# Zero products in an attention's gaps, a fetch of sums put ahead, a flag read early

## The chip, the cores and the metric
One Trainium2 chip, one of its cores. The metric is the device time of one execution in microseconds (us), as the median of several runs. TensorE (PE in the profile) multiplies matrices into PSUM, VectorE (DVE), ScalarE (ACT) and GpSimd (POOL) work on vectors, and SyncE (SP) issues most transfers between HBM and the core's memory.

## The reference
A sparse attention feeds a gated feed-forward layer (FFN 1), and that a second one (FFN 2). All is float32.

```python
scores = scale * np.matmul(q, k.transpose(0, 1, 3, 2))      # batch 4, 8 heads, 576 positions, 64 wide
scores = np.where(masks[None, :, :, :], scores, -1000000000.0)   # window of 32, in half the heads with step 4
...
attn = attn / (np.sum(attn, axis=-1, keepdims=True) + 1e-09)
return np.matmul(attn, v).astype(np.float32)

g = x @ w_gate                                               # 2304 x 512 @ 512 x 1536
silu = g * (1.0 / (1.0 + np.exp(-g)))
val = x @ w_val
return (silu * val @ w_out).astype(np.float32)

h = x @ w_in                                                 # 2304 x 512 @ 512 x 2048
g = h - np.tanh(h)
return (g @ w_out).astype(np.float32)
```

## The kernel before
**Order.** All work is put into a `Plan` as tasks: an engine, an estimated duration, a priority, what it depends on, and the buffers that it needs (rings of a fixed size: eight PSUM buffers `ps`, four of sums `acc`, two of raw weights `st`, six of `q`, eight of `v`). `Plan.order()` plays the tasks through with these estimates: an engine that is free takes the ready task with the lowest priority number whose buffers are free. The result fixes the order of instructions on each engine and in SP's queue, and which buffer each task gets. On the chip each engine then keeps its order and waits by semaphores. A task that is added or gets another dependency can so move others.

**Attention.** 48 units (4 batches, 4 pairs of heads, 3 groups of 192 queries). Each one: loads of q (with k) and v, three score products (L330), maxima and exponentials, normalisation on GpSimd, three transposes (L355), six products with V (L368), and copies into `x`. "Score set 16" is the L330 work of unit 16, and so on. Ten bf16 products of a tile of zeros (`warm_up`, L700) stand ahead of the first unit.

**FFN 1 and 2.** Six tiles of 384 tokens in three pairs. Weights are loaded as 64-bit words and converted (L249 to L265). Each float32 product is made of three products of high and low parts. One pair is done plainly (`plain_up`, L404), two pairs with seven products in place of eight (`product`, L416). Products with the output weights are L582 (FFN 1) and L601 (FFN 2). The hidden width is taken in groups of chunks; after each group, partial sums go to HBM (`add_up`: store by SP or accumulating store by GpSimd). In the last group the sums are fetched back (L539) into an `acc` buffer, VectorE adds the last products to them (L550), and in FFN 2 the result is stored to the output (L614). The last tile's final output is cut in two halves of 256 columns.

**The flag.** FFN 2 uses a cubic in place of h - tanh(h). Whether every value was small enough for that is counted (`count`, `across`, `tell`), and a flag is read into a register on each engine (L883); a branch (L884) leads to `any_size`, which computes FFN 2 again, or past it.

The dependency of the fetch, as it stands:

```python
fetched = plan.add("DMA", 2.0, prio - 6.0, lambda: nc.sync.dma_start(out=at(), in_=keep),
                   [sum_done[t], pieces[0][4][0]], [at], lat=5.0)
```

`pieces[0][4][0]` is the first hidden tile (`y`) of the same token tile: the fetch isn't planned before that is ready.

Of the kernel before, what the change touches and what calls it, by code (L numbers as in the profile page):

```python
# [21 lines left out]
P = 128  # L22
# [145 lines left out]
CONV0 = -18.6  # L168
LEAD = 25.0
DELAY = 10.0  # L170
ON_DVE = {(2, 1)}
DELAY_7 = 6.0
MM = 0.174
QUICK = 0.6
WARM = 10
# [6 lines left out]
def attention_then_two_ffns(ctx, tc, qk, vt, masks, w1, w2, out):  # L182
    nc = tc.nc
# [7 lines left out]
    plan = Plan({r: n for r, (n, _) in SLOTS.items()})  # L191
# [12 lines left out]
    new_ps = ring("ps", [P, 512], F32)  # L204
# [20 lines left out]
    warm = const.tile([P, 512], mybir.dt.bfloat16, name="warm")  # L225
# [168 lines left out]
    covered = {}  # L394
# [136 lines left out]

    sum_done = [None] * NT

    def add_up(layer, t, pieces, first, last, prio):

        at = new_acc()
        keep = sums[layer - 1][t]
        if last:
            fetched = plan.add("DMA", 2.0, prio - 6.0, lambda: nc.sync.dma_start(out=at(), in_=keep),  # L539
                               [sum_done[t], pieces[0][4][0]], [at], lat=5.0)  # L540
        puts = []
        for n, (mm, c0, c1, dur, deps, bufs) in enumerate(pieces):
            ps = new_ps()

            eng = "DVE" if last or (layer, n) in ON_DVE else "ACT"

            def put(ps=ps, c0=c0, c1=c1, eng=eng):
                o = at()[:, c0:c1]
                if last:
                    nc.vector.tensor_tensor(out=o, in0=ps()[:, :c1 - c0], in1=o, op=ALU.add)  # L550
                elif eng == "DVE":
                    nc.vector.tensor_copy(out=o, in_=ps()[:, :c1 - c0])
                else:
                    nc.scalar.activation(out=o, in_=ps()[:, :c1 - c0], func=AF.Copy)  # L554

            a = plan.add("PE", dur, prio, lambda mm=mm, ps=ps: mm(ps), deps, [ps] + bufs)
            c = (c1 - c0) / 1000
            if last:
                a = plan.add("DVE", 0.15 + 1.08 * c, prio, put, [a, fetched], [ps, at])
            else:  # L560
                a = plan.add(eng, 0.15 + 1.08 * c if eng == "DVE" else 0.18 + 0.84 * c, prio, put, [a], [ps, at])
            puts.append(a)
        if last:
            return at, puts

        def store():
            if first:
                nc.sync.dma_start(out=keep, in_=at())
            else:
                nc.gpsimd.dma_start(out=keep, in_=at(), accum_op=ALU.add)  # L570

        sum_done[t] = plan.add("DMA" if first else "POOL", 2.0 if first else 1.3, prio - 5.0, store, puts + [sum_done[t]], [at],
                               lat=8.0)
# [14 lines left out]
                           [w[2][0] for w in ws] + [y for y, _ in ys]))  # L588
        return add_up(1, t, pieces, first, last, prio)

    def ffn2_out(ws, ys, t, first, last, prio, end=False):
        pieces = []
        cuts = [(s, 0, DM) for s in range(NS)]
        if end:
            cuts[-1:] = [(NS - 1, 0, DM // 2), (NS - 1, DM // 2, DM)]
        for s, c0, c1 in cuts:
            def mm(ps, s=s, c0=c0, c1=c1):
                n = 0
                for w, y in zip(ws, ys):
                    for a, bb in PASSES:  # L600
                        nc.tensor.matmul(ps()[:, :c1 - c0], lhsT=y[0]()[:, a, s * P:(s + 1) * P],  # L601
                                         rhs=w[1][0]()[:, bb, c0:c1], start=(n == 0), stop=(n == 3 * len(ws) - 1))
                        n += 1
                covered[ps.slot] = c1 - c0

            pieces.append((mm, s * DM + c0, s * DM + c1, MM * 4 * len(ws) * (c1 - c0) / DM,
                           [d for _, d in ys] + [w[1][1] for w in ws], [w[1][0] for w in ws] + [y for y, _ in ys]))
        r = add_up(2, t, pieces, first, last, prio)
        if last:
            at, puts = r  # L610
            for (s, c0, c1), a in zip(cuts, puts):
                def store(s=s, c0=c0, c1=c1):
                    r0 = t * TT + s * P
                    nc.sync.dma_start(out=out[r0:r0 + P, c0:c1], in_=at()[:, s * DM + c0:s * DM + c1])  # L614

                plan.add("DMA", 0.75 * (c1 - c0) / DM, -1e6, store, [a], [at])
# [53 lines left out]
    def seven_next(p, r, prio):  # L670

        (r1, d1), (r2, d2) = r
        seven_x[p] = sums_x(r1, r2, d1 + d2, None, prio)
# [22 lines left out]
    ps_warm = new_ps()  # L696
# [2 lines left out]
        for _ in range(WARM):  # L699
            nc.tensor.matmul(ps_warm(), lhsT=warm[:, :P], rhs=warm, start=True, stop=True)  # L700

    plan.add("PE", 0.43 * WARM, -1e6, warm_up, bufs=[ps_warm])
    n = 0
    for b in range(B):
        for hp in range(NP):
# [14 lines left out]
    def finish(layer, h, prio):  # L720
        if layer == 1:
            (g, a), v = h
            return times_val(times_gate(g, a, prio), v, prio)
        (h, a), = h
        return cubic(h, a, prio)
# [4 lines left out]
    flag = const.tile([P, 1], mybir.dt.int32, name="flag")  # L730
    when = 0.0
    for layer, sizes in ((1, GROUPS1), (2, GROUPS2)):
        k = 0
        for n in sizes:
            first, last = k == 0, k + n == (NK1, NK2)[layer - 1]
            src, parts = ((w1, 3), (w2, 2))[layer - 1]
            lead = when - LEAD if k or layer == 2 else CONV0
            ups = range(parts - 1)
            sevens = SEVEN if n == 2 else []
            ws = [[None] * parts for _ in range(n)]  # L740
            extra = [None] * parts
            for c in range(parts):
                for i in range(n):
                    ws[i][c] = convert(src[k + i][:, c * 512:(c + 1) * 512], lead + 2 * c, layer == 1 and k == 0)
            for c in ups:
                if sevens:
                    extra[c] = sums_w(ws[0][c], ws[1][c], lead + 6 + 2 * c)
            if layer == 1 and k == 2:
                for p in SEVEN:
                    seven_first(p, when)  # L750
            outp = (ffn1_out, ffn2_out)[layer - 1]
            order = [0, 1, 2] if layer == 1 and not last else [1, 2, 0]
            for p in order:
                tiles = PAIRS[p]
                ys = {t: [] for t in tiles}
                if p in sevens:
                    q = [seven_up(ws[0][c], ws[1][c], extra[c], p, when + 0.01 * c) for c in ups]
                    res = {(i, t): [q[c][2 * i + j] for c in ups] for i in range(2) for j, t in enumerate(tiles)}
                    ys = {t: [None, None] for t in tiles}
                    for i, t in [(0, tiles[0]), (0, tiles[1]), (1, tiles[1]), (1, tiles[0])]:  # L760
                        ys[t][i] = finish(layer, res[i, t], when + 0.02)
                    when += (14.6, 7.3)[layer - 1]
                    for t in tiles:
                        done = outp(ws, ys[t], t, first, last, when + DELAY_7)
                        when += 2.09 * n
                        if last and layer == 1:
                            after[t] = done
                else:
                    for t in tiles:
                        ys = []  # L770
                        for w in ws:
                            ys.append(finish(layer, [plain_up([w], c, t, when)[0] for c in ups], when))
                            when += (4.18, 2.09)[layer - 1]
                        end = {"end": True} if layer == 2 and last and p == order[-1] and t == tiles[-1] else {}
                        done = outp(ws, ys, t, first, last, when + DELAY, **end)
                        when += 2.09 * n
                        if last and layer == 1:
                            after[t] = done
                if last and layer == 1:
                    if p in SEVEN:  # L780
                        seven_next(p, [after[t] for t in tiles], when + DELAY)
                    else:
                        for t in tiles:
                            plain_next(t, after[t], when + DELAY)
            k += n
# [6 lines left out]
    ps_flag = new_ps()  # L792
# [7 lines left out]

    a = plan.add("DVE", 0.4, -1e6, count, squares)
    a = plan.add("PE", 0.3, -1e6, across, [a], [ps_flag])
    plan.add("DVE", 0.1, -1e6, tell, [a], [ps_flag])


    def any_size():
# [73 lines left out]
    with tc.manual_schedule():  # L880
        for t in plan.order():
            t.emit()
        bad = nc.values_load(flag[0:1, 0:1], min_val=0, max_val=1)  # L883
        with tc.If(bad > 0):  # L884
            any_size()


# [48 lines left out]
```

## Time and profile before

| | |
|---|---|
| median of 3 runs | 925.24 us (923.45 to 928.22) |
| the profiled execution | 928.41 us, span 926.3 us from first to last instruction |
| TensorE busy | 904.8 us, 98% of the span |
| VectorE busy | 638.1 us, 69% |
| ScalarE busy | 519.0 us, 56% |
| GpSimd busy | 300.5 us, 32% |
| mean granted TensorE clock | 0.985 of full |
| moved by DMA | 134.55 MB, mean 145 GB/s |

Busy means that an instruction is in flight; matrix products are pipelined, and their ends are modelled. The granted clock is the share of full speed that TensorE was given. The chain of waits, followed back from the last instruction, lies on TensorE for 90% of the span.

### The profile page before, as it was taken

How to read it: one execution, taken by the hardware profiler on the slowest of the kernel's cores; microseconds unless marked ns; L12 is line 12 of the kernel's file. 1: busy time of each engine (PE TensorE's matmuls, PEld its weight loads, DVE VectorE, ACT ScalarE, POOL GpSimd, SP SyncE). 2: the span in 40 equal slices, each digit the busy share in tenths (PEclk: the TensorE clock that was granted, in tenths of full speed). 3: DMA queues.
4: the chain of work that ended last, by engine and by line, in shares of the span. 5: the costliest groups of instructions: out<-in, count | busy, mean ns of one | idle time of the engine just before them, and what ended most of it. 6: DMA issues, size and time to landing. Idle time of an engine off the chain costs nothing.

```text
span 926.3 us, 15209 instructions
## 1 busy us (share of the span) xinstructions
PE 904.8 (98%) x5418; PEld 854.4 (92%) x5418; DVE 638.1 (69%) x1428; ACT 519.0 (56%) x1379; POOL 300.5 (32%) x298
## 2 busy tenths in 40 slices
PE   7899999999999999999999989999999999999996
PEld 6789999999999999999999988899898998999994
DVE  4688888854833833943867998985868585946373
ACT  5598876745645544644655556655656555545430
POOL 2334434314413512522514222242525242521100
PEclk8799999999999999999999999999999999999998
DMA  9887744862672672572581304568685857574756
GB/s 274 233 265 258 252 123 69 204 149 41 141 160 35 137 170 35 128 180 35 115 242 54 114 23 144 197 137 161 140 163 122 165 137 145 106 128 77 171 169 210
DMA packets 38005, 134.55 MB, mean 145 GB/s; under 512 B 4384, under 2 KB 9248, under 8 KB 37920
## 3 DMA queue, kind: packets, MB, share of 16 engines
q0 software_dynamic: 9504, 51.91, 31.4%
q1 hardware_dynamic: 28416, 81.57, 27.5%
q8 instruction: 45, 0.74, 0.3%
q14 instruction: 40, 0.33, 0.1%
HBM read 67.40 MB, written 66.06 MB: 144 GB/s over the span
## 4 chain that ended last, share of the span: by engine, by line
PE 90%; DVE 5%; DMA 3%; SPq 1%; issue 0%; ACT 0%; DVEq 0%
PE ps L416 27%; PE ps L601 21%; PE ps L404 20%; PE ps L582 14%; PE ps L330 3%; PE ps L368 2%; PE ps L355 2%; DMA q<-qk 2%; DVE x L631 1%; DVE acc L550 1%; DVE acc L646 1%; DMA acc<-sum 1%; DVE x L684 0%; DMA st<-w 0%; DVE y L483 0%; DVE t L520 0%
## 5 line engine op out<-in xcount | busy, mean ns | idle before, releaser
L416 PE MATMUL ps<-x,wc 128*128 128x384 f32 x1512 | 279.3, 337 | 0.4 <-DVE acc L550 0.4
L416 PEld LDWEIGHTS ps<-x,wc 128*128 128x128 f32 x1512 | 266.2, 188 | 3.3 <-DVE acc L550 0.7
L237 POOL TENSOR_TENSOR wc<-u,wc 128x512 fp32r<-128x512 f32 x104 | 149.0, 1438 | 224.9 <-ACT wc L234 209.2
L404 PE MATMUL ps<-x,wc 128*128 128x384 f32 x1152 | 210.7, 336 | 0.6 <-DVE t L523 0.6
L601 PE MATMUL ps<-wc,y 128*128 128x512 f32 (+1 forms) x870 | 204.0, 389 | 0.0
L404 PEld LDWEIGHTS ps<-x,wc 128*128 128x128 f32 x1152 | 200.4, 188 | 1.6 <-DVE t L523 0.9
L601 PEld LDWEIGHTS ps<-wc,y 128*128 128x128 f32 x870 | 162.1, 188 | 32.1
L554 ACT ACTIVATE acc<-ps 128x384 f32<-128x384 f32 (+1 forms) x228 | 118.3, 529 | 108.0 <-PE ps L601 56.1
L582 PE MATMUL ps<-y,wc 128*128 128x384 f32 x864 | 159.8, 336 | 1.8 <-DVE acc L550 0.9
L582 PEld LDWEIGHTS ps<-y,wc 128*128 128x128 f32 x864 | 150.5, 188 | 2.8 <-DVE acc L550 1.2
L483 DVE TENSOR_TENSOR y<-t,y 128x384 fp32r<-128x384 f32 x168 | 122.0, 732 | 35.3 <-ACT y L479 34.9
L570 POOL DMA_DIRECT2D sum<-acc x66 | 58.1, 880 | 264.0 <-ACT acc L554 194.5
L234 ACT ACTIVATE wc<-u 128x512 fp32r<-128x512 f32 x104 | 65.5, 630 | 72.3 <-PE ps L416 31.5
L479 ACT ACTIVATE y<-t 128x384 fp32r<-128x384 f32 x168 | 86.2, 519 | 35.2 <-PE ps L601 20.9
L520 DVE SCALAR_TENSOR_TENSOR t<-t 128x384 f32<-128x384 f32 x96 | 63.4, 665 | 29.7 <-ACT t L517 29.7
L456 DVE TENSOR_TENSOR ps<-ps,t 128x384 f32<-128x384 f32 x36 | 20.4, 566 | 65.1 <-PE ps L416 65.0
L252 ACT ACTIVATE u<-st 128x512 f32<-128x512 f32 x68 | 45.2, 667 | 33.3 <-DMA st<-w 32.8
L349 POOL TENSOR_TENSOR e<-e,sm 128x288 f32<-128x288 f32 x48 | 34.4, 720 | 80.0 <-DVE sm L346 27.6
L341 ACT ACTIVATE e<-e,nm 128x96 f32<-128x96 f32 x144 | 52.1, 371 | 8.2 <-DVE nm L335 8.0
L495 DVE SCALAR_TENSOR_TENSOR t<-t,ps 128x384 f32<-128x384 f32 x62 | 34.0, 549 | 28.9 <-ACT t L492 28.4
L427 ACT ACTIVATE ps<-ps 128x384 f32<-128x384 f32 x72 | 34.3, 477 | 34.8 <-PE ps L416 34.7
L260 DVE SCALAR_TENSOR_TENSOR u<-st,u 128x512 uint32<-128x512 uint32 x68 | 53.2, 782 | 0.6
(61 smaller groups left out, 859.5 us busy)
## 6 DMA issues: line engine op xcount, KB each, us to landing
sum<-acc POOLq DMA_DIRECT2D x66, 768.0 KB, 7.1
st<-w SPq DMA_DIRECT2D x68, 512.0 KB, 4.5
q<-qk SPq DMA_DIRECT2D x48, 304.0 KB, 5.1
sum<-acc SPq DMA_DIRECT2D x12, 768.0 KB, 5.6
acc<-sum SPq DMA_DIRECT2D x12, 768.0 KB, 6.1
v<-vt SPq DMA_DIRECT2D x48, 144.0 KB, 4.7
out<-acc SPq DMA_DIRECT2D x17, 256.0 KB, 2.9
mask<-masks SPq DMA_DIRECT2D x1, 288.0 KB, 4.5
```

Of the source, the lines that this page charges most:

```text
L234: nc.scalar.activation(out=w()[:, 0, :], in_=u(), func=AF.Copy)
L237: nc.gpsimd.tensor_tensor(out=w()[:, 1, :], in0=u(), in1=w()[:, 0, :].bitcast(F32), op=ALU.subtract)
L260: nc.vector.scalar_tensor_tensor(out=ui, in0=words(0, U32), scalar=29, in1=ui, op0=ALU.logical_shift_right, op1=ALU.bitwise_or)
L404: nc.tensor.matmul(ps()[:, :TT], lhsT=w()[:, a, kc * P:(kc + 1) * P], rhs=xt[kc // 2]()[:, bb, kc % 2, :], start=(n == 0), stop=(n == 3 * ...
L416: nc.tensor.matmul(ps()[:, :TT], lhsT=w()[:, i, c:c + P], rhs=b()[:, j, k, :], start=(start and n == 0), stop=(n == 5), skip_group_check=True)
L479: nc.scalar.activation(out=y()[:, 0, :], in_=s(), func=AF.Copy)
L483: e.tensor_tensor(out=y()[:, 1, :], in0=s(), in1=y()[:, 0, :].bitcast(F32), op=ALU.subtract)
L520: nc.vector.scalar_tensor_tensor(out=sq(), in0=sq(), scalar=E0 / E1, in1=sq(), op0=ALU.add, op1=ALU.mult)
L554: nc.scalar.activation(out=o, in_=ps()[:, :c1 - c0], func=AF.Copy)
L570: nc.gpsimd.dma_start(out=keep, in_=at(), accum_op=ALU.add)
L582: nc.tensor.matmul(ps()[:, :TT], lhsT=w[2][0]()[:, a, m * P:(m + 1) * P], rhs=y[0]()[:, bb, :], start=(n == 0), stop=(n == 3 * len(ws) - 1))
L601: nc.tensor.matmul(ps()[:, :c1 - c0], lhsT=y[0]()[:, a, s * P:(s + 1) * P], rhs=w[1][0]()[:, bb, c0:c1], start=(n == 0), stop=(n == 3 * le ...
```

## The change
Three things. (1) Thirty tasks `fill` of two products of zeros each (the tile `warm`, into a PSUM buffer that nobody reads) are added to TensorE's plan with the highest priority number, each dependent on the one before; the plan puts one wherever it sees TensorE without other work. (2) In FFN 2's last group, the fetch of a tile's sums no longer depends on that tile's own first `y`, but on the first `y` of the pair that was done before (`early`). (3) The flag is read into registers in a task of the plan, right behind `tell`; the branch stays at the end.

```diff
+FILL = 30
...
-    def add_up(layer, t, pieces, first, last, prio):
+    def add_up(layer, t, pieces, first, last, prio, early=None):
...
             fetched = plan.add("DMA", 2.0, prio - 6.0, lambda: nc.sync.dma_start(out=at(), in_=keep),
-                               [sum_done[t], pieces[0][4][0]], [at], lat=5.0)
+                               [sum_done[t], early or pieces[0][4][0]], [at], lat=5.0)
...
-    plan.add("PE", 0.43 * WARM, -1e6, warm_up, bufs=[ps_warm])
+    ps_warmed = plan.add("PE", 0.43 * WARM, -1e6, warm_up, bufs=[ps_warm])
...
+            early = None
             for p in order:
...
+                    now_early = ys[tiles[0]][0][1]
                     for t in tiles:
-                        done = outp(ws, ys[t], t, first, last, when + DELAY_7)
+                        more = {"early": early} if layer == 2 and last else {}
+                        done = outp(ws, ys[t], t, first, last, when + DELAY_7, **more)
...
+                if p in sevens:
+                    early = now_early
...
-    plan.add("DVE", 0.1, -1e6, tell, [a], [ps_flag])
+    a = plan.add("DVE", 0.1, -1e6, tell, [a], [ps_flag])
+    verdict = []
+    plan.add("NONE", 0.0, -1e6, lambda: verdict.append(nc.values_load(flag[0:1, 0:1], min_val=0, max_val=1)), [a])
+
+
+    a = ps_warmed
+    for _ in range(FILL):
+        ps = new_ps()
+
+        def fill(ps=ps):
+            for _ in range(2):
+                nc.tensor.matmul(ps(), lhsT=warm[:, :P], rhs=warm, start=True, stop=True)
+            covered[ps.slot] = 512
+
+        a = plan.add("PE", 0.46, 1e6, fill, [a], [ps], lat=0.5)
...
-        bad = nc.values_load(flag[0:1, 0:1], min_val=0, max_val=1)
-        with tc.If(bad > 0):
+        with tc.If(verdict[0] > 0):
             any_size()
```

Where the instructions stand. Numbers behind a name tell buffers in use apart and differ between the two kernels; line numbers of the changed kernel are one higher from L331 on, and its fills are L822.

TensorE in the attention, before the change: from score set 15 to score set 19 (L330), with the transposes of units 10 and 11 (L355) and the V products of unit 10 (L368) between them.

```order
L330 MATMUL ps_512<-q_466 128x96 x3
L355 MATMUL ps_527<-ident,e_456 96x128 x3
L330 MATMUL ps_543<-q_485 128x96 x3
L368 MATMUL ps_561<-at_550,v_347 64x64 x6
L330 MATMUL ps_570<-q_508 128x96 x3
L330 MATMUL ps_590<-q_540 128x96 x3
L355 MATMUL ps_599<-ident,e_502 96x128 x3
L330 MATMUL ps_603<-q_552 128x96 x3
```

The same place after the change: score sets 16 to 18 (L331). Just ahead of these rows stand the V products of units 9 and 10 and two more fills, just behind them one more fill and the transposes of unit 11.

```order
L331 MATMUL ps_580<-q_520 128x96 x3
L822 LDWEIGHTS warm
L822 MATMUL ps_598<-warm 128x512
L822 LDWEIGHTS warm
L822 MATMUL ps_598<-warm 128x512
L331 MATMUL ps_607<-q_548 128x96 x3
L822 LDWEIGHTS warm
L822 MATMUL ps_617<-warm 128x512
L822 LDWEIGHTS warm
L822 MATMUL ps_617<-warm 128x512
L331 MATMUL ps_623<-q_577 128x96 x3
```

Each score set from 16 to 18 now has a fill behind it, and V set 10 has moved ahead of score set 16. Thirteen fills stand between score sets 2 and 19; between score sets 13 and 15 there is none.

TensorE at the boundary of the layers, before: FFN 1's last seven-product blocks (L416) and the output products behind them (L582).

```order
L416 MATMUL ps_6120<-x_5882,wc_6055 128x384 x6
L416 MATMUL ps_6095<-x_5886,wc_5647 128x384 x6
L416 MATMUL ps_6134<-x_5985,wc_5822 128x384 x6
L582 MATMUL ps_6168<-y_6052,wc_5392 128x384 x3
L582 MATMUL ps_6168<-y_6132,wc_5607 128x384 x3
```

After, the same L417 products (L416 before):

```order
L822 LDWEIGHTS warm
L822 MATMUL ps_6187<-warm 128x512
L417 MATMUL ps_6137<-x_5925,wc_5686 128x384 x6
L417 MATMUL ps_6182<-x_6024,wc_5861 128x384 x6
L822 LDWEIGHTS warm
L822 MATMUL ps_6213<-warm 128x512
L822 LDWEIGHTS warm
L822 MATMUL ps_6213<-warm 128x512
```

Three fills now stand ahead of these two blocks and two behind them; nine in all at this boundary, six of them ahead of the L582 products above.

SP's queue at the end, before: fetches of sums (L539) and stores of the output (L614); `acc_9742` is the last tile's.

```order
L614 DMA out<-acc_9497 128x512 x2
L614 DMA out<-acc_9431 128x512
L539 DMA acc_9603<-sum 128x1536
L614 DMA out<-acc_9431 128x512 x2
L539 DMA acc_9633<-sum 128x1536
L614 DMA out<-acc_9497 128x512
L614 DMA out<-acc_9603 128x512 x2
L614 DMA out<-acc_9633 128x512 x2
L614 DMA out<-acc_9557 128x512 x3
L539 DMA acc_9742<-sum 128x1536
```

After (L540 and L615; `acc_9717` is the last tile's, `acc_9696` the one that was `acc_9603`):

```order
L540 DMA acc_9567<-sum 128x1536
L615 DMA out<-acc_9567 128x512 x2
L615 DMA out<-acc_9497 128x512 x3
L540 DMA acc_9696<-sum 128x1536
L615 DMA out<-acc_9567 128x512
L540 DMA acc_9717<-sum 128x1536
L615 DMA out<-acc_9696 128x512 x2
L813 TENSOR_LOAD flag
L813 ISA x2
L615 DMA out<-acc_9531 128x512 x2
```

The last fetch now stands behind six stores, before behind thirteen; the fetch for the sum that the next products belong to stands behind five, before behind three. The flag's read stands among the stores. On TensorE it stands two output pieces of FFN 2 behind `across` and eight ahead of the end, where it was last before; three fills stand ahead of the run of output pieces that ends the program, two ahead of the last tile's four, and three behind them.

## Rows read from the trace of the kernel before

**Rows 1.** Busy time by stage: stretch, length, busy per engine, PEclk, DMA share, GB/s.
```profile
11.40:18.20 6.80, 6.08 (x37) 5.54 (x37) 3.70 (x28) 3.93 (x19) 2.80 (x5) 0.50 1.04 298
...
28.00:35.20 7.20, 4.49 (x50) 3.57 (x48) 5.32 (x37) 4.43 (x22) 4.06 (x4) 1.00 0.96 276
35.20:48.90 13.70, 12.55 (x81) 11.57 (x81) 7.43 (x49) 6.58 (x33) 4.07 (x5) 0.50 0.66 206
48.90:145.00 96.10, 95.93 (x964) 88.98 (x961) 80.09 (x388) 79.44 (x343) 38.45 (x46) 1.00 0.71 218
...
500.00:556.00 56.00, 53.29 (x300) 51.83 (x299) 55.66 (x90) 32.64 (x65) 14.74 (x11) 1.00 0.18 57
...
880.00:917.00 37.00, 37.00 (x186) 32.73 (x184) 24.69 (x49) 10.27 (x29) 0.00 (x0) 1.00 0.66 214
```

**Rows 2.** Waits of SP's DMA queue, 35 to 50 us: total, times, longest.
```profile
SPq L372 <- PE ps L368: 10.0, 3, 4.9
```

**Rows 3.** TensorE in order of time, attention: start, length, idle before.
```profile
36.35 1.57 PE L330 MATMUL ps<-q 128*128 128x96 f32 x6 [1.37 <-DMA q<-qk]
```

**Rows 4.** The chain that ended last, in order of time: start, length, what.
```profile
38.76 2.81 PE ps L330 x12
...
44.71 0.84 PE ps L368 x12
45.55 0.81 PE ps L355 x3
...
68.76 0.64 PE ps L330 x6
69.40 0.50 PE ps L368 x12
69.90 0.46 PE ps L355 x3
...
852.54 12.28 PE ps L601 x54
```

**Rows 5.** The tile of zeros: duration min/median/max in ns, first and last start.
```profile
L700 PE MATMUL ps<-warm x10: 379/634/634, 1.2 to 4.8; 128*128 128x512 bf16 x10
```

**Rows 6.** TensorE in order of time at the boundary of the layers.
```profile
537.68 1.33 PE L582 MATMUL ps<-y,wc 128*128 128x384 f32 x6 [0.88 <-DVE t L523]
...
540.97 1.32 PE L582 MATMUL ps<-y,wc 128*128 128x384 f32 x6 [0.91 <-DVE acc L550]
```

**Rows 7.** The chain that ended last, its end.
```profile
900.36 5.49 PE ps L601 x24
...
911.34 6.33 DMA acc<-sum
...
918.95 0.75 DVE acc L550 x2
```

**Rows 8.** All engines in order of time from 880 us.
```profile
894.29 0.37 SPq L539 DMA_DIRECT2D acc<-sum  x1
...
900.87 0.33 SPq L539 DMA_DIRECT2D acc<-sum  x1
...
901.29 10.00 SPq L614 DMA_DIRECT2D out<-acc  x8
...
905.83 11.25 PE L601 MATMUL ps<-wc,y 128*128 128x512 f32 x54
```

**Rows 9.** Line 883, the flag's read: duration in ns, first and last start.
```profile
L883 PEldq TENSOR_LOAD <-flag x1: 516/516/516, 914.1 to 914.1; - x1
...
L883 SPq TENSOR_LOAD <-flag x1: 485/485/485, 920.6 to 920.6; - x1
```

**Rows 10.** Line 884, the branch and the waits after it.
```profile
L884 SPq EVENT_SEMAPHORE  x8: 17/17/17, 924.1 to 924.6; - x8
...
L884 SPq COMPARE_BRANCH  x1: 50/50/50, 921.5 to 921.5; - x1
```

**Rows 11.** Line 614 from 919.8 us, the last two stores.
```profile
DMA to landing us min/median/max: 3.6/3.7/3.8
```

More of the change, by code (lines that the diff above doesn't have):

```diff
@@ L589, in ffn1_out, with ffn2_out @@
         return add_up(1, t, pieces, first, last, prio)
-    def ffn2_out(ws, ys, t, first, last, prio, end=False):
+    def ffn2_out(ws, ys, t, first, last, prio, end=False, early=None):
         pieces = []
@@ L607, in ffn2_out @@
                            [d for _, d in ys] + [w[1][1] for w in ws], [w[1][0] for w in ws] + [y for y, _ in ys]))
-        r = add_up(2, t, pieces, first, last, prio)
+        r = add_up(2, t, pieces, first, last, prio, early)
         if last:
@@ L773, in attention_then_two_ffns @@
                             when += (4.18, 2.09)[layer - 1]
-                        end = {"end": True} if layer == 2 and last and p == order[-1] and t == tiles[-1] else {}
-                        done = outp(ws, ys, t, first, last, when + DELAY, **end)
+                        more = {"early": early} if layer == 2 and last else {}
+                        if layer == 2 and last and p == order[-1] and t == tiles[-1]:
+                            more["end"] = True
+                        done = outp(ws, ys, t, first, last, when + DELAY, **more)
                         when += 2.09 * n
```

## The prediction
> **What bounds the kernel now.** I read the busy time by stage first [rows 1]. From 48.9 us on, TensorE has something in flight practically all the time at the full granted clock: 95.93 of 96.10 us up to 145 us and 37.00 of 37.00 at the end; of the later stages only 500 to 556 us shows a gap, 53.29 of 56.00 us. What TensorE is given there is paid in full, except in that gap. The reader should look at two other rows of the group. In the attention the clock is granted at 0.50 of full (1.2 of 2.4 GHz) twice, from 11.4 to 18.2 us and from 35.2 to 48.9 us. The first costs nothing that I can find: the DMA share there is 1.04, transfers set the pace, and TensorE still waits for them later. The second is different. The DMA share drops to 0.66, although loads for the scores are still to come. The DMA queue's own waits say why: it stands 10.0 us behind the products with V that free a V buffer [rows 2]. TensorE at half clock is the bound there, and everything later hangs on it.
>
> What TensorE did before that fall is the row of 28.0 to 35.2 us in [rows 1]: busy 4.49 of 7.20 us, with short waits for q such as the 1.37 us at 36.35 [rows 3].
>
> Then the chain of work at either level [rows 4]: two sets of scores take 2.81 us at half clock, one takes 0.64 at full; a set of products with V 0.84 and 0.50; a set of transposes 0.81 (in others 0.64) and 0.46. Last come the end's rows [rows 7 to 11].
>
> **The change part by part.**
>
> *Price of one fill.* A fill is two bf16 products of 512 columns. The ten warm-up products start between 1.2 and 4.8 us, 0.40 us apart [rows 5]; the full-clock price is that of the 512-column L601 products, 12.28 us for 54, 0.227 each [rows 4]. So a fill is 0.46 us at full clock and 0.80 us at the slow pace. In the order, thirty fills fall as 13 in the attention, 9 at the boundary of the layers, 5 ahead of the last outputs, and 3 after the last output product.
>
> *Attention, if the clock stays up.* The chain from 36.35 to 49.05 us holds six sets of scores (8.1 us in all), three sets of products with V (2.5) and three sets of transposes (2.1). At the full-clock prices that is 3.9, 1.5 and 1.4 us: 5.9 us less. Can the transfers feed that? They run at 276 GB/s before the fall and 206 in the slow stretch [rows 1], so 0.96 MB, or 3.5 us of transfer, is lost in those 13.7 us; it comes back if V buffers are freed sooner. Against it stand the fills. The first eight and the two ahead of score set 16 lie in waits for q; three more lie between score set 16 and the transposes after set 18, 1.4 us, hidden only where TensorE waits for q. Ends: -5.9 (all hidden) and -4.5 (three paid); I take -4.6, since TensorE shows next to no wait after set 16 today, so only a transfer that is late for the faster TensorE could hide them. If the cover is gone and the clock falls anyway, the five fills from set 16 on cost 0.80 each, 4.0 us, less the 1.37 us of wait: +2.6.
>
> Does the clock stay up? The fills do not lie evenly in the stretch that goes before the fall: between score sets 13 and 15 there is none; two follow just before set 16. One thing helps besides: in the new order two loads (V 14 and q 15) pass the third weight load, so score set 15 comes sooner. I give 6 to 7 in 10 that the slow stretch goes, and 2.5 in 10 that it comes but ends sooner, since a fill at the slow pace is 0.80 us without a break.
>
> *Boundary of the layers.* Nine fills, 4.1 us. TensorE's gaps there are 2.7 us in all (56.00 - 53.29), the longest 0.88 and 0.91 us, both for VectorE [rows 6], which is busy 55.66 of 56.00 us [rows 1]. Six fills stand ahead of the first of them, so they eat it and delay TensorE into the next. If VectorE loses nothing by that, 4.1 - 2.7 = 1.4 us remain; if TensorE's delay reaches VectorE's operands each time, all 4.1. I take +1.8, near the lower end because VectorE's queue is full of work that does not depend on these products (a row with 0.34 us of idle time). The clock is 1.00 here already: there is nothing to win.
>
> *End, TensorE.* Five fills ahead of the last outputs, in a stretch without a gap [rows 1]: paid, +2.3 us (0 only if the new order leaves them a wait; today's has none). The flag's read now stands in the middle of TensorE's output products. Its queue took 0.52 us for it at 914.1 us [rows 9] while products ran to 905.83 + 11.25 = 917.08 [rows 8], so the queue issues some 3 us ahead, and a pause of 0.5 us alone should not reach the array. Bounds 0, and 0.52 plus what the flag is late: I take +0.5, the flag being late for the reason below. The Trainium skill (TensorE: Matmul & The Clock Gate, architectural detail on the array, engine queue depths) gives TensorE a queue of 64 against 8 elsewhere. By that the read would cost nothing; the trace's lead of 3 us agrees.
>
> *End, the early fetch.* Today the sixth and last fetch of sums goes at 911.34 us and lands 6.33 us later; the last additions end at 918.95 + 0.75 = 919.70 [rows 7], while the last product ends at 917.08. In the new order it stands behind six stores instead of thirteen and takes the buffer of the sixth's sum. That store goes at about 901.29 [rows 8]; a landing takes 3.6 to 3.8 us [rows 11]; so the fetch goes at about 905.5 and is there at 912, before it is needed. The additions then end some 0.6 us after the last product, 917.7 instead of 919.70: -2.0. What is late next? The sum that the next products belong to, fetched fourth at 894.29 today, becomes the fifth, which waits for a store to land and goes at 900.87 [rows 8]. With 6.3 us it lands at 907, while its first products (six take 1.37, 5.49 / 4 [rows 7]) are done at 900.36 + 1.4 + 1.4 = 903.1. VectorE stands up to 4 us, and behind it the flag and the other additions; TensorE has eight PSUM buffers, and VectorE's 0.7 us per addition against 1.37 of products catches up before the last tile. Cost 0 beyond the 0.5 above, or up to 1 if a PSUM buffer lacks.
>
> *End, the flag.* On SP the read starts at 920.6 us [rows 9] and the branch at 921.5; the eight waits after it run from 924.1 to 924.6 [rows 10]. Without the read the branch comes 0.86 us sooner, and the waits with it, the last at 923.8. The last two stores go at 919.5 and 920.0 and land 3.6 to 3.8 us later [rows 11], 923.8 at the latest, so nearly the whole comes: -0.86 (0 if the landing were later). The 2.6 us between branch and waits stay, as the branch stays. The Trainium skill (Runtime: NRT & Kernel Launch, instruction fetch mechanics) says that a taken branch out of the fetched pages waits for its target to be fetched; the 2.6 us agree with that. The three fills after the last product delay TensorE's branch alone, by 1.4 us, and SP ends later than that.
>
> *Sum.* -4.6 + 1.8 + 2.3 + 0.5 - 2.0 - 0.86 = -2.9 us. The profiled execution took 928.41 us (span 926.3), so 925.5 by its own time; it lies 3.2 us above the median of 925.24. Off the median, which is what is compared, that is **922.4 us**. The runs' spread (923.45 to 928.22) is as large as the first term; if it is the slow clock in differing lengths, the median has less to win than this profile.
>
> **The rivals.**
> A. *All fills in waits.* The clock holds, the three attention fills and the five at the end are hidden, the boundary costs 1.4, the flag's read nothing: -5.9 + 1.4 - 2.0 - 0.86 = -7.4, 917.9 us. For it: loads can become the bound again after 36 us. Against: [rows 1] show no gap at the end.
> B. *The slow stretch comes but is cut short.* Half of 5.9 is won, three fills paid at 0.46 to 0.80: about -1.2; with the rest (+1.7) +0.5, 925.7 us: no change. The change then doesn't do what it says.
> C. *The other side: fills paid at half clock.* The clock falls at 35 us as today, because no fill lies between score sets 13 and 15, and stays low to 48.9: +2.6 in the attention, +1.7 for the rest, and up to 2.3 more with the boundary at its upper end: +4.3 to +6.6, 929.5 to 931.8 us. It decides from the point where attention and boundary together cost 4.7 us (the end gives back 0.06). For it: the uneven placing. Against: five fills are 4 us of dense work in the very stretch in which the clock has to rise.
>
> **How the numbers follow.** Forecast (clock holds, most fills paid) 0.45; A 0.20; B 0.25; C 0.10. Half a per cent, 4.6 us, is about what a measurement of this kernel can tell from no change: the borders are 920.6 and 929.9. A is faster throughout, and about a third of the forecast's own range (919.7 to 925: the start between -5.9 and -3.5, the boundary between 1.4 and 3); B is same; C is slower in most of its range. Faster 0.35, same 0.57, slower 0.08. The range goes from 917 (A with a little less lost at the boundary) to 928 (B with the boundary at its worst).
>
> **What would show it.** Clock: 1.00 granted in 35.2 to 48.9 us, the DMA share there near 0.9. Boundary: VectorE still full, TensorE's gaps gone, the stretch longer by 1 to 3 us. End: no wait of VectorE for the last fetch, one for the fifth, the last addition 0.6 us after the last product, SP's 2.6 us behind the branch unchanged. The prediction is wrong if the clock falls at 35 us with the fills in place, if TensorE stops at the flag's read, or if the later fifth fetch holds TensorE up for a PSUM buffer.

## The result, and the profile after

| | before | after |
|---|---|---|
| median | 924.87 us of 8 runs (923.20 to 928.22) | 930.38 us of 8 runs (928.61 to 933.71) |
| ratio | | 1.0063 [1.0041, 1.0085] |
| the profiled execution | 928.41 us, span 926.3 | 930.73 us, span 928.6 |

A ratio is that of the times, this kernel over the kernel before in runs taken together with it, with a 95% interval in brackets. The changed kernel is slower by 0.63%, where 922.4 us and no more than 928 were forecast. Its page says that TensorE has 5.5 us more in flight than before (904.8), and GpSimd, ScalarE and VectorE about the same as before:

```profile
span 928.6 us, 15321 instructions
...
PE 910.3 (98%) x5471; PEld 852.6 (92%) x5478; DVE 639.1 (69%) x1428; ACT 516.3 (56%) x1379; POOL 299.9 (32%) x298
```

The busy time by stage of the changed kernel, in the stretches and with the columns of [rows 1]:

```profile
28.00:35.20 7.20, 6.50 (x70) 4.68 (x70) 5.84 (x28) 2.83 (x10) 2.87 (x3) 1.00 0.99 278
35.20:48.90 13.70, 12.62 (x113) 10.89 (x114) 10.97 (x72) 12.50 (x69) 7.05 (x8) 1.00 0.90 283
48.90:145.00 96.10, 94.83 (x948) 88.12 (x947) 80.40 (x373) 76.60 (x322) 39.54 (x46) 1.00 0.68 209
500.00:556.00 56.00, 56.00 (x317) 53.48 (x318) 54.94 (x89) 33.01 (x65) 14.35 (x12) 1.00 0.14 49
880.00:917.00 37.00, 36.95 (x184) 32.29 (x184) 26.77 (x52) 11.92 (x35) 0.00 (x0) 1.00 0.63 216
```

The clock is granted in full from 35.2 to 48.9 us, the DMA share there is 0.90, the boundary's gaps are gone. All that was forecast, and the first product of FFN 1 (L405) indeed starts at 45.58 us instead of 50.99. So the question is where 5.4 us went that had been won by then. To see it, each kernel's products (the zeros left out) were added up at their full-clock durations, and the moment was read at which each had done the same amount; the difference, after less before, is

| moment in the kernel before | 62.6 us | 102.2 | 140.9 | 180.8 | 459.6 | 499.6 | 583.3 | 904.3 | end of the span |
|---|---|---|---|---|---|---|---|---|---|
| after less before, us | -5.1 | -5.8 | -4.2 | **+1.3** | +1.3 | +2.2 | +3.0 | +4.2 | +2.3 |

Between 140.9 and 180.8 us, in FFN 1, 5.45 us go at one place. TensorE's waits in the changed kernel (total, times, longest) name it:

```profile
PE ps L331 <- DMA q<-qk: 5.8, 11, 2.1
PE ps L583 <- ACT acc L555: 3.6, 1, 3.6
...
PE ps L369 <- DVE t L496: 1.1, 1, 1.1
PE ps L583 <- DVE t L505: 0.6, 1, 0.6
PE ps L602 <- DVE t L524: 0.4, 1, 0.4
```

None of the last four rows is among the kernel before's waits. The row of L505 stands at 463 us and is the step from +1.3 to +2.2, that of L524 at 562.8 us the one to +3.0. The second row is the large one. The chain that ended last, in order of time, shows what stands behind it:

```profile
155.63 2.61 PE ps L583 x15
...
158.26 0.50 ACT acc L555
158.76 0.29 issue
159.06 9.38 DMA sum<-acc
...
168.54 0.50 ACT acc L555
...
169.08 1.48 PE ps L583 x6
170.56 5.59 PE ps L405 x24
```

An accumulating store (L571, GpSimd) of a buffer of sums is issued at 159.06 us and lands 9.38 us later. ScalarE's next copy of a finished product writes into that very buffer. In the order of time on ScalarE it stands idle 6.04 us:

```profile
168.54 1.64 ACT L555 ACTIVATE acc<-ps 128x384 f32<-128x384 f32 x4 [6.04 <-DMA sum<-acc]
```

The PSUM buffers behind it aren't freed, so TensorE's L583 waits 3.57 us. And it is not only the wait. Busy time by stage, the same columns, around it, first two rows of the kernel before, then the changed kernel:

```profile
160.00:170.00 10.00, 10.00 (x59) 10.00 (x58) 7.74 (x11) 8.36 (x18) 3.92 (x4) 1.00 0.78 206
170.00:174.00 4.00, 4.00 (x25) 4.00 (x24) 2.68 (x4) 1.42 (x5) 1.18 (x1) 1.00 0.54 205
```

```profile
160.00:170.00 10.00, 6.43 (x37) 6.11 (x36) 7.40 (x9) 3.62 (x8) 1.28 (x1) 1.00 0.63 134
170.00:174.00 4.00, 4.00 (x16) 4.00 (x15) 1.21 (x2) 3.71 (x9) 3.03 (x3) 0.57 0.48 197
174.00:180.00 6.00, 6.00 (x37) 6.00 (x36) 5.69 (x10) 3.69 (x8) 1.40 (x2) 1.00 0.78 131
```

Right behind the wait the granted clock is 0.57 over four microseconds: 16 products where the kernel before has 25. Wait (3.57) and half clock (3.4 us at half speed, 1.7 lost) make 5.3 of the 5.45 us.

At the end, the changed kernel in order of time, all engines:

```profile
906.79 0.33 SPq L540 DMA_DIRECT2D acc<-sum  x1
907.21 16.57 SPq L615 DMA_DIRECT2D out<-acc  x13
...
908.52 8.46 PE L602 MATMUL ps<-wc,y 128*128 128x512 f32 x36
...
917.51 4.55 PE L602 MATMUL ps<-wc,y 128*128 128x512 f32 x24
...
922.09 0.42 DVE L551 TENSOR_TENSOR acc<-ps,acc 128x256 f32<-128x256 f32 x1 [0.29 <-PE ps L602]
```

The last fetch goes at 906.79 us, before at 911.34 [rows 7]; the last addition ends at 922.51, 0.45 us after the last product (922.06), before 2.62. The flag's read and the branch, by line (duration in ns, first and last start):

```profile
L813 SPq TENSOR_LOAD <-flag x1: 1608/1608/1608, 908.9 to 908.9; - x1
...
L813 PEldq TENSOR_LOAD <-flag x1: 1714/1714/1714, 908.9 to 908.9; - x1
```

```profile
L905 SPq EVENT_SEMAPHORE  x8: 17/17/17, 926.4 to 926.9; - x8
...
L905 SPq COMPARE_BRANCH  x1: 50/50/50, 923.8 to 923.8; - x1
```

The read takes 1.7 us on TensorE's queue, three times that of [rows 9], yet the L602 products around it run on without a gap.

### The profile page after: what moved, and what is told of

Read it like the earlier page. It is cut to its first block, busy times and chain, and to the rows that moved or that the text cites. A ratio compares the mean times of both kernels' runs of the same rounds, so it can differ in the third digit from the quotient of the medians.

```text
span 928.6 us, 15321 instructions
## 1 busy us (share of the span) xinstructions
PE 910.3 (98%) x5471; PEld 852.6 (92%) x5478; DVE 639.1 (69%) x1428; ACT 516.3 (56%) x1379; POOL 299.9 (32%) x298
## 4 chain that ended last, share of the span: by engine, by line
PE 93%; DMA 4%; DVE 1%; SPq 0%; issue 0%; ACT 0%; ACTq 0%
PE ps L417 28%; PE ps L602 21%; PE ps L405 21%; PE ps L583 16%; DMA q<-qk 3%; PE ps L331 2%; PE ps L369 2%; PE ps L356 1%; DMA sum<-acc 1%; PE ps L822 1%; DVE sm L346 0%; SPq L373 0%; SPq L372 0%; DVE t L521 0%; DVE u L257 0%
## 5 line engine op out<-in xcount | busy, mean ns | idle before, releaser
L417 PE MATMUL ps<-x,wc 128*128 128x384 f32 x1512 | 280.1, 337 | 0.0
L417 PEld LDWEIGHTS ps<-x,wc 128*128 128x128 f32 x1512 | 266.1, 188 | 3.5
L405 PE MATMUL ps<-x,wc 128*128 128x384 f32 x1152 | 212.2, 338 | 0.0
L602 PE MATMUL ps<-wc,y 128*128 128x512 f32 (+1 forms) x870 | 205.3, 390 | 0.4 <-DVE t L524 0.4
L405 PEld LDWEIGHTS ps<-x,wc 128*128 128x128 f32 x1152 | 202.2, 189 | 0.7
L602 PEld LDWEIGHTS ps<-wc,y 128*128 128x128 f32 x870 | 161.9, 188 | 33.0 <-DVE t L524 0.7
L583 PE MATMUL ps<-y,wc 128*128 128x384 f32 x864 | 160.8, 337 | 4.2 <-ACT acc L555 3.6
L583 PEld LDWEIGHTS ps<-y,wc 128*128 128x128 f32 x864 | 150.4, 188 | 5.3 <-ACT acc L555 3.9
L571 POOL DMA_DIRECT2D sum<-acc x66 | 58.3, 883 | 266.5 <-ACT acc L555 194.9
L484 DVE TENSOR_TENSOR y<-t,y 128x384 fp32r<-128x384 f32 x168 | 119.1, 714 | 35.7 <-ACT y L480 35.5
L457 DVE TENSOR_TENSOR ps<-ps,t 128x384 f32<-128x384 f32 x36 | 20.4, 566 | 66.2 <-PE ps L417 66.2
L496 DVE SCALAR_TENSOR_TENSOR t<-t,ps 128x384 f32<-128x384 f32 x62 | 34.1, 549 | 29.9 <-ACT t L493 29.3
L257 DVE TENSOR_SCALAR u<-u 128x512 uint32<-128x512 uint32 x68 | 42.9, 636 | 15.8 <-ACT u L253 15.7
```

Of the source, the lines that this page charges most:

```text
L405: nc.tensor.matmul(ps()[:, :TT], lhsT=w()[:, a, kc * P:(kc + 1) * P], rhs=xt[kc // 2]()[:, bb, kc % 2, :], start=(n == 0), stop=(n == 3 * ...
L417: nc.tensor.matmul(ps()[:, :TT], lhsT=w()[:, i, c:c + P], rhs=b()[:, j, k, :], start=(start and n == 0), stop=(n == 5), skip_group_check=True)
L484: e.tensor_tensor(out=y()[:, 1, :], in0=s(), in1=y()[:, 0, :].bitcast(F32), op=ALU.subtract)
L583: nc.tensor.matmul(ps()[:, :TT], lhsT=w[2][0]()[:, a, m * P:(m + 1) * P], rhs=y[0]()[:, bb, :], start=(n == 0), stop=(n == 3 * len(ws) - 1))
```

## The experiments

The theory: the fills are placed by the plan, so they move its other work too; in the new order a buffer of sums is taken again while its store is still under way, and that wait, with the clock's fall behind it, is most of the loss. The rivals: the fills' own time; the new end; a clock that the fills don't hold.

**No fill.** The changed kernel with

```diff
-FILL = 30
+FILL = 0
```

> The changed kernel without its thirty fills: the order of before, but for the last group's end. Theory (the fetch and the flag's read work as worked out; the loss is elsewhere): about 2.9 us under before, 922.0. Rival (the later fifth fetch or the flag's read in mid-stream takes back what the sixth fetch gives): within 0.5 us of before, 924.9.

Measured 921.91 us, ratio 0.9965 [0.9950, 0.9980]. Order and waits of the attention are those of before, and the slow clock is back, in its busy time by stage:

```profile
28.00:35.20 7.20, 5.82 (x57) 4.79 (x58) 5.73 (x38) 5.74 (x27) 3.58 (x4) 0.80 1.02 312
35.20:48.90 13.70, 13.49 (x101) 12.39 (x98) 7.79 (x52) 7.87 (x42) 3.80 (x5) 0.61 0.62 193
```

The half clock lasts 13.65 us as in the kernel before, but from 32.4 to 46.0 us, and this execution is 2.9 us ahead from there on with the same instructions. The place of the slow stretch is not fixed. The new end is worth 0.35%; the loss is the fills'.

**The order alone.** The changed kernel, every fill planned, none emitting its products:

```diff
         def fill(ps=ps):
-            for _ in range(2):
-                nc.tensor.matmul(ps(), lhsT=warm[:, :P], rhs=warm, start=True, stop=True)
-            covered[ps.slot] = 512
+            pass
```

> The changed kernel with every instruction in its place, but the thirty fills emit no products, so that only the order differs from before, and the clock is left to itself. Theory (the new order of the plan makes TensorE wait for a buffer of sums at about 165 us, whenever it comes there): that wait of some 3.6 us is there, 929 to 931 us in all, the slow clock in the attention as before. Rival 1 (TensorE, no longer slow, runs into a store that isn't through; the order has nothing to do with it): no such wait, 922 to 924. Rival 2 (it is the fills' own time that costs): 922 to 924 too.

Measured 924.43 us, ratio 1.0001 [0.9982, 1.0020]. Without one product of zeros, TensorE still waits for the sums:

```profile
PE ps L583 <- ACT acc L555: 2.1, 1, 2.1
```

and the clock falls behind it, in the busy time by stage:

```profile
170.00:174.00 4.00, 4.00 (x18) 4.00 (x18) 1.47 (x3) 3.62 (x9) 3.30 (x3) 0.70 0.51 201
```

The lead over before goes from -2.9 us at 140.9 to +1.0 at 180.8. So the new order by itself makes the wait and loses the lead. The time is not the 929 to 931 us that was expected: the changed kernel, with the products, takes 0.62% more. Earlier the lead had been -5.7 us, as large as with the zeros, although the clock was at half for 6.8 us (35.9 to 42.7). Whether the new order brought it is not shown: the profile of the fetch alone (below) has the same lead in the old order.

**Zeros in the old order.** The kernel before, with two zero products ahead of 20 score sets, into the PSUM buffer that the scores then overwrite, so that the plan sees no new task:

```diff
+            if 2 <= unit < 2 + FILL:
+                for _ in range(2):
+                    nc.tensor.matmul(ps(), lhsT=warm[:, :P], rhs=warm, start=True, stop=True)
```

> The kernel before in its own order; two products of zeros stand ahead of each of the score sets 3 to 22, in the PSUM buffer that the scores then overwrite, so no task is added. Theory (order): the clock stays up in 35 to 49 us, 5 to 6 us are won there and kept, 919 to 920 us. Rival 1 (running into the store): won and given back near 165 us, 924 to 926. Rival 2 (fills' own time): twenty fills of 0.46 us are paid, 924 or more.

Measured 924.01 us, ratio 0.9983 [0.9971, 0.9995]. The clock is 1.00 throughout the attention:

```profile
35.20:48.90 13.70, 13.60 (x130) 11.50 (x132) 10.41 (x67) 10.41 (x56) 5.63 (x8) 1.00 0.89 281
```

The lead against the profile of before is -3.6 us at 102.2 and still there at 459.6, with no wait for sums; at the end of the span -1.9 is left. By the ratio the gain is 0.17%, 1.6 us, not the 5 to 6 us that were expected. What rival 1 needs, a loss near 165 us, isn't there; rival 2's number (924 or more) came, but that it is the fills' own time is not shown. The profile that it is held against had lost more to its slow stretch than the four other profiles of this order without zeros (no fill, flag alone, fetch alone, planned landing without fills): at 62.6 us they are 2.0 to 5.8 us ahead of it.

**Thirteen fills**, those of the attention:

```diff
-FILL = 30
+FILL = 13
```

> The changed kernel with the first 13 fills alone: FFN 1 in the changed order, FFN 2 in the order of before with the new end. Theory (order): the wait near 165 us stays, only what the boundary's and the end's fills cost goes, 2 to 3 us: 927.5 to 928.5. Rival 2 (the fills' own time): 17 fills less, 6.4 us less: 924.

Measured 927.83 us, ratio 1.0027 [1.0009, 1.0044]. The wait is there, with 6.8 us of half clock from within it on (168.5 to 175.3 us), and the lead falls from -3.5 to +2.9:

```profile
PE ps L583 <- ACT acc L555: 3.5, 1, 3.5
```

The 17 later fills make the rest of the way to 1.0063: 0.36%, 3.3 us.

**The store left out.** The changed kernel, all 30 fills, with the one accumulating store of 159 us not issued:

```diff
+            if at is plan.accs[6]:
+                return
```

> The changed kernel, all thirty fills in place, without one of its 66 accumulating stores: the one at 159 us whose buffer of sums TensorE's products wait for (so a partial sum of one tile is left out). Every other instruction stands where it stood. Theory (the order reuses that buffer before its store has landed, and the pause then lowers the clock): the wait of 3.6 us and the slow clock after it go, about 5.4 us: 924.5 to 925.5. Rival (another wait takes its place, or it is the fills): 929 or more.

Measured 925.28 us, ratio 1.0008 [0.9991, 1.0026]: 0.55% or 5.1 us less than the changed kernel. Around the place TensorE has no gap and the full clock:

```profile
160.00:170.00 10.00, 10.00 (x59) 10.00 (x59) 9.58 (x12) 7.34 (x16) 5.52 (x4) 1.00 0.43 120
170.00:174.00 4.00, 4.00 (x25) 4.00 (x24) 4.00 (x7) 3.64 (x7) 0.88 (x1) 1.00 0.62 126
```

The order is otherwise the changed kernel's, so this one store holds the 5 us.

**Zeros in the old order, and the new end.** The third kernel with the changed kernel's fetch and flag, its fills written in place of the tasks:

```diff
-FILL = 30
+FILL = 0
...
+            if 2 <= unit < 22:
+                for _ in range(2):
+                    nc.tensor.matmul(ps(), lhsT=warm[:, :P], rhs=warm, start=True, stop=True)
```

> The order of before with the new end (early fetch, flag read ahead), and products of zeros ahead of score sets 3 to 22 in the scores' own PSUM. Theory: the two gains add, -0.9 and -3.1: 921 us. Rival (both cut into the same slack): 922 or more, no better than the new end alone.

Measured 921.11 us, ratio 0.9959 [0.9944, 0.9975]. By itself the new end had 0.9965 and the zeros 0.9983: the zeros add little to the new end, and the intervals can't tell it from nothing.

**The flag alone**, in the kernel before:

```diff
-    plan.add("DVE", 0.1, -1e6, tell, [a], [ps_flag])
+    a = plan.add("DVE", 0.1, -1e6, tell, [a], [ps_flag])
+    verdict = []
+    plan.add("NONE", 0.0, -1e6, lambda: verdict.append(nc.values_load(flag[0:1, 0:1], min_val=0, max_val=1)), [a])
...
-        bad = nc.values_load(flag[0:1, 0:1], min_val=0, max_val=1)
-        with tc.If(bad > 0):
+        with tc.If(verdict[0] > 0):
```

> The kernel before with only the flag's read moved behind its making. Theory: 0.9 us from SP's tail, less what the read costs in mid-stream, 924.0 to 924.5; the two microseconds more of the new end belong to the early fetch. Rival (the tail hangs on the last stores' landing, or TensorE stops at the read): 925 or more.

Measured 924.39 us, ratio 0.9995 [0.9979, 1.0011]: less than can be measured, and neither 0 nor 0.86 us is excluded.

**A plan that knows the landing.** Thirteen fills, and a buffer of sums of FFN 1 counts as free only 7 us after the 1.3 us that its accumulating store has in the plan (stores of that stage land in 6.6 to 9.4 us; the edit holds the buffers of the first group's plain stores too), so that the plan puts other work there:

```diff
+HOLD = 7.0
-FILL = 30
+FILL = 13
...
+            if isinstance(t, Buf):
+                self.free[t.ring].append(t.slot)
+                continue
...
-                    self.free[b.ring].append(b.slot)
+                    if t.hold:
+                        heapq.heappush(events, (now + t.hold, -2 - t.n, b))
+                    else:
+                        self.free[b.ring].append(b.slot)
...
-                               lat=8.0)
+                               lat=8.0, hold=HOLD if layer == 1 else 0.0)
```

> The changed kernel with 13 fills, and a plan that counts a buffer of sums in FFN 1 as free only 7 us after its accumulating store, as long as a landing takes; the attention's order stays as changed. Theory (the plan gives the buffer away too early): no wait of TensorE for a buffer of sums, the lead of some 5 us of the attention kept: 919 to 921. Rival (with a buffer less, TensorE waits elsewhere in FFN 1): 925 or more.

Measured 919.76 us, ratio 0.9946 [0.9930, 0.9963]: faster than before, and than the changed kernel. The wait is gone and the lead of -4.5 us at 140.9 is still -4.5 at 180.8:

```profile
160.00:170.00 10.00, 10.00 (x59) 10.00 (x58) 9.78 (x12) 8.57 (x18) 6.12 (x4) 1.00 0.84 231
170.00:174.00 4.00, 4.00 (x25) 4.00 (x24) 4.00 (x7) 0.32 (x1) 0.00 (x0) 1.00 0.94 193
```

**The fetch alone.** The kernel before with `early` for the fetch of sums, and the flag read at the end:

```diff
-                               [sum_done[t], pieces[0][4][0]], [at], lat=5.0)
+                               [sum_done[t], early or pieces[0][4][0]], [at], lat=5.0)
```

> The kernel before with only the early fetch: no fills, the flag read at the end as before. Fetch and flag together gave a ratio of 0.9965, the flag alone 0.9995. Theory (the fetch is what shortens the end): 0.9970, within 0.996 and 0.998, that is 2 to 3.5 us less, and the last addition 0.6 to 1 us behind the last product in the trace. Rival (the two only help together, since the flag's read behind the last stores sets the end once the fetch is early): 0.999 or more.

Measured 923.09 us, ratio 0.9984 [0.9969, 0.9999]: 1.5 us, somewhat under what was expected. The last addition ends 0.46 us after the last product. This execution also shows the old attention order with a much shorter slow stretch (3.4 us instead of 13.65), by stage:

```profile
28.00:35.20 7.20, 5.18 (x50) 4.61 (x49) 5.55 (x37) 4.35 (x21) 3.90 (x4) 0.83 1.00 301
35.20:48.90 13.70, 13.15 (x127) 12.01 (x127) 9.61 (x68) 11.96 (x64) 5.35 (x8) 0.96 0.85 272
```

It is 5.8 us ahead of the profile of before at 102.2 us, as far as the changed kernel, without a single fill.

**The planned landing without fills**: the same, with

```diff
-FILL = 13
+FILL = 0
```

> As the planned-landing kernel, but with no fill at all: the attention's order and the slow clock as before, the new end, and a plan that counts a buffer of sums as free 7 us behind its accumulating store. Theory (the zeros and the order they bring are worth something once the store's wait is gone): about as the new end alone, ratio 0.9965, within 0.9955 and 0.998, so 1 to 3 us behind the planned landing with 13 fills (0.9946). Rival (what made the planned landing fast is the plan, not the fills): 0.995 or less, the same as with 13 fills.

Measured 922.71 us, ratio 0.9971 [0.9952, 0.9989], about the new end alone (0.9965). What the plan's knowledge brings, it brings to the order with fills. By medians 13 fills are 3 us better than none, by the ratios 2.3 us, but the intervals (0.9946 up to 0.9963, 0.9971 down to 0.9952) overlap, so that much is not shown. One of its twelve executions had a mean granted clock of 0.999 and took 916.78 us, the least of all runs of this study; the other eleven had 0.985 to 0.995 and took 919.26 to 924.51.

**The planned landing with all 30 fills:**

```diff
-FILL = 13
+FILL = 30
```

> The changed kernel with all 30 fills and the plan that knows the landing. Theory (the store's wait is the greater part of what the changed kernel lost, and the 17 fills behind the attention cost some 2 to 3 us): no wait of TensorE for the sums near 165 us, 922 to 924 us, ratio 0.9965 to 0.999. Rival (the later fills disturb more than their own time, or the wait comes back elsewhere): 926 us or more, ratio over 1.001.

Measured 925.43 us, ratio 1.0008 [0.9991, 1.0025]. The wait is gone here too, and the time is that of the kernel with the store left out, 925.28. It lies between what the two theories expected: the 17 later fills cost 0.62% against 13 fills, 5.7 us by the ratios. The two profiles put less of that on the fills: of 4.9 us between their ends 1.3 are there before 499.6 us, where none of the 17 stands, 0.7 come at the boundary, 2.1 ahead of the last outputs and 0.8 behind the last product. That is 3.6 us, and by their own time it would be 3.7: 14 fills of 0.46 us less the boundary's 2.7 us of gaps (three stand behind the last product).

## Why the prediction was wrong

The terms, against the shifts in the table of the result:

| term | predicted, us | measured in the profiles, us |
|---|---|---|
| attention, to 140.9 us | -4.6 (-5.9 to -4.5) | -5.8 at its best, -4.2 left |
| FFN 1 behind it | 0 (not in the sum) | **+5.45** at 165 us, +0.9 at 463 us |
| boundary of the layers | +1.8 | +0.7 |
| end: five fills and the flag's read | +2.3 + 0.5 | +2.0 |
| early fetch, flag, SP's tail | -2.86 | -2.7 |
| sum, against the profiled execution | -2.9 | +2.3 |

The last two measured rows are worked out so: TensorE's last product ends at 922.06, before at 917.08, which is 2.0 us more than the +3.0 after the boundary; from there the span goes on for 6.5 us, before 9.2.

**The step that failed** is in the first paragraph: from 48.9 us on, "What TensorE is given there is paid in full, except in that gap." That read the later stages as the same work plus fills. But a fill is a task of the plan, and the tasks behind the attention came in another order, as the section on the kernel says that they can. The prediction looked at the order in three places and costed the rest at nothing; none of its rivals had a store that comes late. That the order does it, the fills without products show (the wait without zeros) and zeros in the old order (no wait); that this one store holds 5 us, the kernel without it shows; that it is the plan's freeing of a buffer ahead of the landing, the planned landing shows. From no fill (0.9965) to 30 fills (1.0063) it is 0.98%, 9.1 us: the one store is 0.55% of that, a little over half, and the 17 later fills are 0.36%.

**The attention's clock.** The mechanism was right: 1.00 in the stretch, DMA share 0.90 near the forecast 0.9. The gain was of the forecast size against the profile, but that is an execution with a late, long slow stretch, and the same lead came without zeros too: -5.7 us in the new order (fills without products, 6.8 us of half clock) and -5.8 in the old (fetch alone, 3.4 us). So the profiles don't tell what the zeros' part is and what the order's. Nor did the fills keep the clock up everywhere: in the profiles of thirteen fills, the store left out and the planned landing it is at half for 3.4 us between 23.7 and 28.7 us, and in that of the planned landing with 30 fills from 8.4 to 11.8. The prediction had said that the median might have less to win than the profile; it then took the whole -4.6 off the median all the same. The old order shows 13.65 us of half clock in four profiles and 3.4 us in a fifth. How much of the attention's gain is left against the median stays open: 1.6 us (0.5 to 2.7) for zeros in the old order, 2 to 3 us or nothing for fills and their order, by the overlap above.

**From -5.8 to -4.2.** Between 102 and 141 us the new order loses 1.6 us again, 1.06 of it in the wait of L369 for VectorE's L496 that the waits show; the kernels with empty fills and with 13 show the same wait, the kernel before doesn't have it. This term was not in the sum either.

**Boundary.** Nine fills, 4.1 us, cost 0.7, below the lower bound of 1.4: the room was larger than the 2.7 us of idle time that the prediction took off. From 520 to 560 us the kernel before took 40.0 us for products that make 35.9 at their full-clock spacing, as idle time counts only from the modelled end of a product, 0.34 us behind its start, while in dense work the next starts after 0.17. By 560 us the changed kernel is again +2.2 us behind, as ahead of the boundary. The 0.7 come right after, in the wait of L602 for L524, and VectorE was held up ahead of it: its L457 stood 0.93 and 0.80 us for products of L417 at 556.5 and 560.0 us, before 0.25 and 0.12. So TensorE's delay did reach VectorE, at the end and at a small price.

**End.** The five fills cost 2.0 us, near the 2.3 taken; the flag's read cost TensorE nothing, where 0.5 was taken for a flag that is late. No wait of VectorE for the fifth fetch came. Fetch, flag and SP's tail gave 2.7 of the 2.86 us, and 0.35% by the ratio without fills. SP's 2.6 us from the branch to its waits (923.8 to 926.4) are unchanged, as forecast. But the branch itself comes 1.8 us behind the last product, with the planned landing and 13 fills 0.9: there the last addition releases SP's last store, here the last but one, and the last goes 0.66 us behind it. That is the plan's order once more.

## What to carry to other kernels

Work that is put into a planner can move all the work behind it: compare the whole order, and for each buffer that is used again ask when its last transfer lands, not when it was issued. A plan that frees a buffer at the issue of a store is right only as long as the order happens to leave time; giving the plan the landing (here 7 us) turned 0.3% slower into 0.5% faster with the same 13 fills. And before a gain is read from one profile, see whether the stage lasts the same in other executions of the kernel.

## What the runs showed of the hardware

A wait of TensorE inside dense work can cost more than its length: behind 3.57 us of it the granted clock was 0.5 for 3.4 us, behind 2.1 us (empty fills) 3.4 us, from within 3.5 us (13 fills) on 6.8 us; the boundary's waits of up to 0.91 us [rows 6] have none behind them, nor have those of 1.0 to 1.1 us near 113 us (L369 and L496). In between it differs from execution to execution: in the attention a wait for q of 2.1 us (changed kernel, up to 24.4 us) had none behind it, waits of 1.8, 1.9 and 2.7 us at the same place (store left out, planned landing, 13 fills) had 3.4 us.

The slow stretch of the old attention order differs from execution to execution: it starts between 30.4 and 35.3 us and lasts 3.4 or 13.65 us. Over 86 executions of the kernel before, the mean granted clock is 0.983 to 0.993, and an execution is 0.56 us longer for each 0.001 less (correlation -0.74). The two kernels with zeros in the old order stay between 0.995 and 0.999, and their two profiles show no half clock from 5.1 us to the end of the work. Yet the zeros bring only 0.17% (0.05 to 0.29). By the fit above 0.01 of clock would be 5 to 6 us; that the zeros' own time (an estimate: 20 pairs of 0.46 us, 9 us, in part in waits) eats the difference is likely, but no run shows it.

The same read of a flag took 0.49 to 0.72 us where each queue read at its own time at the end, and 1.6 to 1.75 us on five queues at once in the middle, and TensorE's products did not pause for it.
